# Attention and a routed MoE in one kernel: another cut of the queries, and the second pair's rows made by VectorE instead of TensorE

## The chip, the cores and the metric

The kernel runs on one core of one Trainium2 chip. The time is device time in microseconds, from runs of the whole kernel. Before the change three runs gave 729.36, 731.09 and 735.09 us; the median, 731.09 us, is the time the prediction starts from. One further execution was profiled. It took 731.5 us, of which the trace covers a span of 729.8 us from the first to the last instruction.

The core has five engines that run their own instruction streams in order and wait for one another through semaphores: TensorE (PE in the profile; its weight loads are PEld), VectorE (DVE), ScalarE (ACT), GpSimd (POOL) and SyncE (SP), which issues most DMA transfers.

## The reference

Two blocks follow each other. First attention with a sliding window of 128 keys and a linear distance bias, for 8 batches, 8 heads, 576 positions and head size 64:

```python
scores = scale * np.matmul(q, k.transpose(0, 1, 3, 2))
mask = (rel >= 0) & (rel < window)
scores = np.where(mask, scores + bias[None], -1000000000.0)
attn = np.exp(scores - np.max(scores, axis=-1, keepdims=True))
attn = attn / (np.sum(attn, axis=-1, keepdims=True) + 1e-09)
return np.matmul(attn, v)
```

The result, as 4608 token rows of 512 values, goes through a mixture of experts: a gate picks one of 8 experts for each token, `relu(x @ w1[e]) @ w2[e]` is computed with the picked expert's weights (512 to 1024 to 512), and the row is scaled by the softmax weight of the pick. All of it is in 32-bit floats.

## The kernel before

**Stages.** In the trace, attention takes about the first 178 us; the rest is the experts, one after another. The change lies wholly in attention. The experts need a token's row from main memory (`x_rows`), from which GpSimd gathers the rows of each expert.

**Units and steps.** Attention is cut into 16 units. A unit is a pair of batches and a pair of heads; four units with the same two batches follow each other, and these four are called a pair here (pair 1 is units 0 to 3, pair 2 is units 4 to 7, and so on; in the code `bp` counts them from 0). A unit has 576 queries and keys, that is nine blocks of 64. It is worked off in four steps `g` = 0 to 3, so the main loop (L1389) has 64 steps `i`.

**Scores.** `scores(i)` (L777) handles two key blocks (three in the last step of a unit). TensorE multiplies keys with the up to three query blocks that can see them (L785) into one of two PSUM buffers `sp`; four 64x64 quarters of the array work side by side. ScalarE takes the exponential (L794 for the outer query blocks, L804 for the inner one), and VectorE multiplies the outer part by a precomputed factor of the distance (L798). The product `pe` has six buffers. `scores_to(n)` runs scores up to index n - 1; the main loop keeps it four steps ahead (three in the first two units).

**Values and sums.** `values(u, half, kbs)` (L815) multiplies `pe` by the values (L828) into the accumulator `at`. A unit's queries are taken in two halves, which `QH` (L578) defines: the first five blocks, then the other four. There is a single `at` buffer, so the second half can start only when ScalarE has copied the first away (L845, in `finish`, L836). `finish` also has TensorE form the rows' sums by multiplying `pe` with an indicator (L859) into a buffer `m`, which ScalarE copies or VectorE adds (L870) to `sumT`. `m` has two buffers, which the gates, the transposes and the routing use too.

**The order of a step.** The program order is written out by hand in the main loop (`tc.manual_schedule`); the planner does not move work between steps. Before the change:

- step 0: scores, values of key blocks 0 and 1, a task;
- step 1: values 2 and 3, a task, scores;
- step 2: values 4, finish of the first half, a task, scores, values 3 to 5 of the second half;
- step 3: values 6 to 8, finish of the second half, a task, scores.

**Tasks.** When a pair has been through attention, its gate, routing and rows are made behind the next pair's attention. `behind(bp)` (L1340) returns a list of tasks, and `some()` (L1370) runs one item of it a step. An item can have several parts. Among these parts: `gate` (TensorE and VectorE), `turn` (TensorE transposes, ScalarE copies), `scale_a` to `scale_c` and `count` (VectorE), `place`, `place2`, `ones_at`, `ones_at2`, `enlist` (mostly VectorE), and the rows. In units 10 and 11 every step also runs one of eight VectorE sums of the first expert's weights (`ws_tasks`, L1422, the sums themselves at L530 to L533).

**Rows, two ways.** A pair has 9 row tiles of 128 tokens. Attention's result `xT` lies by column, the row in memory has four pieces of 132 values (128 and 4 scale factors).

1. `row_turned` and `row_out` (L1064, L1073): TensorE transposes four 128x128 blocks (L1067) into `m`, ScalarE copies them to `xs` (L1069), GpSimd adds the scale factors (L1076) and stores the tile with one DMA (L1081; two for the ninth tile).
2. `squares_turned`, `squares_scaled`, `squares_out` (L1116, L1123, L1128): VectorE turns the tile in squares of 32x32 (L1118), GpSimd copies the scale factors (L1126) and stores the tile with four DMAs, one for each 32 partitions (L1137; eight for the ninth tile). The scale factors have first to be brought into the order of the squares, once a pair, by `scales_squared` (L1096 on TensorE, copies on ScalarE).

`xs` has four buffers for both ways (`rows`, L520). Before the change pair 1 uses the second way, pairs 2 and 3 the first, and pair 4, behind the first expert, the second with most stores on SyncE. The ninth tile of pair 1 is made in the third item of pair 2's list.

```python
            ahead = i + (3 if u < 2 else 4)
            if g == 0:
                scores_to(ahead)
```

Of the kernel before, what the change touches and what calls it, by code (L numbers as in the profile page):

```python
# [458 lines left out]
def kernel(  # L459
# [12 lines left out]
    nc = tc.nc  # L472
# [9 lines left out]
    KB = P // 2  # L482
    NK = S // KB
    BP = N // S // 2
    TPB = 2 * S // P
# [21 lines left out]
    with ExitStack() as fast:  # L507
# [70 lines left out]
        QH = [(0, 5 * KB), (5 * KB, 4 * KB)]  # L578
# [761 lines left out]
        def behind(bp):  # L1340
# [10 lines left out]
            if bp == 0:  # L1351
                rt = [lambda t=t: squares_turned(bp, t) for t in range(TPB)]
                ro = [
                    lambda t=t: (squares_scaled(bp, t), squares_out(bp, t, nc.gpsimd)) for t in range(TPB)
                ]
                return [g3[0:1], g3[1:2], g3[2:] + t3[0:1], t3[1:], a, a2, b, b2, c + n, rt[0:1], q + p + rt[1:2],
                        p2 + rt[2:4] + ro[0:2], o + ro[2:4], o2, rt[4:6] + ro[4:5], e + rt[6:8] + ro[5:8]]
            rt, ro = ([lambda t=t, f=f: f(bp, t) for t in range(TPB)] for f in (row_turned, row_out))
            if bp == 1:
                last = [lambda: squares_turned(0, TPB - 1), lambda: squares_scaled(0, TPB - 1),  # L1360
                        lambda: squares_out(0, TPB - 1, nc.gpsimd)]
                return [g3[0:1], g3[1:2], g3[2:] + t3[0:1] + last, t3[1:], a + rt[0:1], a2 + rt[1:2], b + rt[2:3],
                        b2 + rt[3:4], c + n, [], p + ro[0:2], p2 + ro[2:4] + rs[4:5], o + rs[5:6], o2 + rs[6:7], rs[7:8],
                        e + rs[8:9]]
            return [g3, t3, a + a2, b + b2 + rt[0:1], c + n + rt[1:2], rt[2:4], p + p2 + ro[0:4], o + o2 + rs[4:6],
# [23 lines left out]
        for i in range(NG):  # L1389
            u, g = divmod(i, 4)  # L1390
            bp, hp = units[u]
# [13 lines left out]
            if g == 0:  # L1405
                scores_to(ahead)
            if g == 0:
                values(u, 0, (0, 1))
                if u < HP - 1:
                    factors(u + 1)  # L1410
            elif g == 1:
                values(u, 0, (2, 3))
            elif g == 2:
                values(u, 0, (4,))
                finish(u, 0)
                some()
                scores_to(ahead)
                values(u, 1, (3, 4, 5))
            else:
                values(u, 1, (6, 7, 8))  # L1420
                finish(u, 1)
# [5 lines left out]
            if g != 2:  # L1427
                some()
            if g in (1, 3):
                scores_to(ahead)  # L1430
# [322 lines left out]
```

## Time and profile before

| what | value |
|---|---|
| median of three runs | 731.09 us |
| profiled execution | 731.5 us, span 729.8 us |
| TensorE busy | 672.8 us, 92% of the span |
| VectorE busy | 360.8 us, 49% |
| ScalarE busy | 214.0 us, 29% |
| GpSimd busy | 237.2 us, 32% |
| mean granted TensorE clock | 0.966 of full speed |
| data moved | 122.01 MB, 167 GB/s on average |

The busy time of an engine is the time in which one of its instructions runs. The table shows averages over stages that have different limits, so a stage has to be looked at by itself. In the listings by time, a line has the start in us, the duration in us, the engine, the line of the kernel, the operation, what it writes and reads, the shape, how many neighbouring instructions are merged (x40), and in square brackets the idle time of the engine ahead of it and what ended that. A 32-bit matmul shows up as two records, so x16 are eight matmuls. An instruction's end on TensorE is modelled, and neighbours overlap a little; what a stretch of work costs there is best read from its start to the start of the next stretch.

### The profile page before, as it was taken

How to read it: one execution, taken by the hardware profiler on the slowest of the kernel's cores; microseconds unless marked ns; L12 is line 12 of the kernel's file. 1: busy time of each engine (PE TensorE's matmuls, PEld its weight loads, DVE VectorE, ACT ScalarE, POOL GpSimd, SP SyncE). 2: the span in 40 equal slices, each digit the busy share in tenths (PEclk: the TensorE clock that was granted, in tenths of full speed). 3: DMA queues.
4: the chain of work that ended last, by engine and by line, in shares of the span. 5: the costliest groups of instructions: out<-in, count | busy, mean ns of one | idle time of the engine just before them, and what ended most of it. 6: DMA issues, size and time to landing. Idle time of an engine off the chain costs nothing.

```text
span 729.8 us, 14663 instructions
## 1 busy us (share of the span) xinstructions
PE 672.8 (92%) x6004; PEld 551.9 (76%) x6004; DVE 360.8 (49%) x727; ACT 214.0 (29%) x493; POOL 237.2 (32%) x372
## 2 busy tenths in 40 slices
PE   6899899998999849998999799989997998999996
PEld 5678678686888738876878587868786977788893
DVE  3447758673895537422833372347236531842500
ACT  5767467673321211022103111211121021102310
POOL 8000753042025720255027312722271247022020
PEclk9999999999999969998999899989999999999998
DMA  9878988665089603662285318442833472366010
GB/s 267 207 198 250 283 214 264 196 216 165 13 208 335 211 22 116 208 239 53 108 287 169 123 44 285 158 141 72 306 98 130 159 270 55 116 212 222 1 58 8
DMA packets 63167, 122.01 MB, mean 167 GB/s; under 512 B 5905, under 2 KB 29489, under 8 KB 63090
## 3 DMA queue, kind: packets, MB, share of 16 engines
q1 hardware_dynamic: 51138, 92.51, 40.0%
q0 software_dynamic: 10800, 27.58, 12.2%
q8 instruction: 49, 0.80, 0.5%
q10 hardware_dynamic: 1152, 0.88, 0.4%
q14 instruction: 28, 0.23, 0.1%
HBM read 101.79 MB, written 19.96 MB: 167 GB/s over the span
## 4 chain that ended last, share of the span: by engine, by line
PE 61%; issue 19%; another core or an unknown queue 5%; POOL 5%; DVE 3%; ACT 2%; DMA 1%; SPq 0%; POOLq 0%; ACTq 0%; DVEq 0%
PE sp L785 5%; PE at L828 4%; PE pair0b L1558 4%; PE pair0a L1558 4%; PE pair1a L1558 4%; PE pair1b L1558 3%; PE pair0a L1501 3%; POOL xg L1271 3%; PE pair2b L1501 3%; PE pair2a L1501 3%; PE pair0b L1501 3%; PE pair2a L1558 3%; PE pair1a L1501 2%; PE pair2b L1558 2%
## 5 line engine op out<-in xcount | busy, mean ns | idle before, releaser
L1581 POOL DMA_INDIRECT out_dram<-zo,s_idx x39 | 44.4, 1139 | 294.7 <-DVE zo L1572 193.1
L1271 POOL DMA_INDIRECT xg<-x_rows,p_idx x124 | 123.8, 999 | 37.8 <-issue 36.9
L798 DVE TENSOR_TENSOR pe<-pe,fac 128x512 f32<-128x512 f32 x64 | 43.7, 687 | 52.5 <-ACT pe L794 52.5
L785 PE MATMUL sp<-q_sb,k_sb 64*64 64x192 f32 (+2 forms) x1152 | 56.4, 323 | 10.7 <-DMA q_sb<-in_qT_dram 5.3
L828 PE MATMUL at<-pe,v_sb 64*64 64x192 f32 (+2 forms) x1408 | 58.6, 289 | 3.9 <-issue 3.6
L828 PEld LDWEIGHTS at<-pe,v_sb 64*64 64x64 f32 x1408 | 48.3, 137 | 13.9 <-issue 7.9
L785 PEld LDWEIGHTS sp<-q_sb,k_sb 64*64 64x64 f32 x1152 | 40.6, 137 | 19.8 <-issue 8.6
L794 ACT ACTIVATE pe<-sp 128x512 f32<-128x512 f32 x64 | 38.5, 602 | 38.3 <-issue 18.1
L1512 ACT ACTIVATE h<-h 128x512 f32<-128x512 f32 x32 | 20.2, 630 | 89.7 <-DVE h L1511 81.2
L804 ACT ACTIVATE pe<-sp,mid 128x128 f32<-128x128 f32 x128 | 40.2, 374 | 0.0
L859 PE MATMUL m<-pe,ind 128*32 128x192 f32 (+2 forms) x704 | 29.6, 287 | 1.6 <-issue 0.9
L1137 POOL DMA_DIRECT2D x_rows<-xs x48 | 25.9, 549 | 10.3 <-DVE at_col L1023 2.4
L859 PEld LDWEIGHTS m<-pe,ind 128*32 128x32 f32 x704 | 23.2, 110 | 4.0 <-issue 1.1
L1283 DVE TENSOR_TENSOR xn<-xg 128x512 f32<-128x512 f32 x39 | 26.0, 668 | 0.0
L1558 PE MATMUL pair1b<-w,h 128*128 128x256 f32 x72 | 20.2, 405 | 6.1 <-issue 5.9
L1299 DVE STREAM_TRANSPOSE xgT<-xn 128x512 f32<-128x512 f32 x31 | 22.1, 711 | 1.1
L1558 PEld LDWEIGHTS pair1b<-w,h 128*128 128x128 f32 x72 | 14.1, 198 | 10.2 <-issue 8.5
L538 DVE TENSOR_TENSOR w2s<-w 128x512 f32<-128x512 f32 x16 | 10.9, 684 | 21.2 <-DMA w<-in_moe_w_dram 21.2
L845 ACT COPY xT<-at 128x640 f32<-128x640 f32 (+1 forms) x32 | 18.9, 592 | 8.3 <-PE at L828 7.2
L1613 PE MATMUL pair2a<-w,h 128*128 128x512 f32 x48 | 21.1, 592 | 0.0
L1558 PE MATMUL pair2b<-w,h 128*128 128x256 f32 x56 | 16.4, 420 | 4.4 <-issue 4.3
L1558 PE MATMUL pair0b<-w,h 128*128 128x256 f32 x64 | 17.9, 419 | 2.1 <-issue 1.9
(378 smaller groups left out, 1393.4 us busy)
## 6 DMA issues: line engine op xcount, KB each, us to landing
w<-in_moe_w_dram SPq DMA_DIRECT2D x29, 2048.0 KB, 8.0
k_sb<-in_kT_dram SPq DMA_DIRECT2D x15, 576.0 KB, 6.0
q_sb<-in_qT_dram SPq DMA_DIRECT2D x15, 576.0 KB, 6.8
v_sb<-in_v_dram SPq DMA_DIRECT2D x30, 288.0 KB, 4.5
x_rows<-xs POOLq DMA_DIRECT2D x16, 264.0 KB
x_rows<-xs POOLq DMA_DIRECT2D x32, 66.0 KB
x_rows<-xT SPq DMA_DIRECT2D x8, 264.0 KB, 5.8
w<-in_moe_w_dram SPq DMA_DIRECT2D x4, 512.0 KB, 9.4
```

The source lines that it names most:

```text
L785: nc.tensor.matmul(by_distance(sp[c * KB : (c + 1) * KB, r, :GC], kb, 0, n), lhsT=k_sb[u][hs, c, kb * KB : (kb + 1) * KB], rhs=q_sb[u][hs, ...
L794: nc.scalar.activation(outer, sp[:, :, :GC].rearrange("p r (j x) -> p r j x", j=3)[:, :, 0:3:2, :], AF.Exp, scale=SCALE,)
L798: nc.vector.tensor_tensor(outer, outer, fac[:, h0 : h0 + 2, : 2 * w].rearrange("p r (j x) -> p r j x", j=2)[:, :, :, : 2 * KB], op=ALU.mult,)
L804: nc.scalar.activation(pe[:, r, inner], sp[:, r, inner], AF.Exp, bias=mid[:, h0 + r : h0 + r + 1], scale=SCALE,)
L828: nc.tensor.matmul(acc[r * D : (r + 1) * D, c, lo - q0 : hi - q0].rearrange("p (j x) -> p j x", x=KB), lhsT=v_sb[u][c * KB : (c + 1) * KB, ...
L859: nc.tensor.matmul(sm[32 * j : 32 * j + 32, lo - q0 : hi - q0].rearrange("p (j x) -> p j x", x=KB), lhsT=none[:] if pe is None else ind[:, ...
L1137: eng.dma_start(x_d[r0 : r0 + n * m, a * PW : (a + 1) * PW].rearrange("(k i) w -> i k w", i=TQ), xs[a * TQ : (a + 1) * TQ, p0 // TQ : p0 / ...
L1271: nc.gpsimd.indirect_dma_start(out=to, out_offset=None, in_=where, in_offset=bass.IndirectOffsetOnAxis(ap=idx, axis=0),)
L1283: nc.vector.tensor_tensor(xn[:], x, s.unsqueeze(3).to_broadcast([P, NA, HP, TQ]), op=ALU.mult)
L1501: nc.tensor.matmul(ps[:, f * 256 : (f + 1) * 256], lhsT=left[m][:, d, fb * P : (fb + 1) * P], rhs=right[m][:, d, :], start=(m in (1, 2, 5) ...
L1558: nc.tensor.matmul(ps[:, :256], lhsT=left[m][:, f, c * P : (c + 1) * P], rhs=right[m][:, f, :], start=(m in (1, 2, 5) and f == 0), stop=Tr ...
L1581: ins = nc.gpsimd.indirect_dma_start(out=out[:, :], out_offset=bass.IndirectOffsetOnAxis(ap=s_idx[:, g["c0"] + j : g["c0"] + j + 1], axis= ...
```

## The change

Three things change together.

1. The halves are cut elsewhere: the first half has four query blocks, the second five. The first half needs key blocks 0 to 3 and is finished in step 1; the second needs 2 to 8. The number of matmuls and their shapes stay the same in sum.
2. The scores of two steps stand directly behind one another: at the end of step 1 and the start of step 2, and at the end of step 3 and the start of the next step 0. Before, only the latter two were neighbours. A task now runs after all other work of its step, ahead of the scores at the step's end.
3. Pair 2's rows are made the second way, with the same list as pair 1's: no TensorE transposes and ScalarE copies for them, in their place `scales_squared`, VectorE's turns and four GpSimd stores a tile. The eight turns of tiles 1 to 8 fall in units 10 and 11. The ninth tile of pairs 1 and 2 is made in the first item of the next pair's list.

```diff
-        QH = [(0, 5 * KB), (5 * KB, 4 * KB)]
+        QH = [(0, 4 * KB), (4 * KB, 5 * KB)]
...
-            if bp == 0:
+            last = [lambda: squares_turned(bp - 1, TPB - 1), lambda: squares_scaled(bp - 1, TPB - 1),
+                    lambda: squares_out(bp - 1, TPB - 1, nc.gpsimd)] if bp else []
+            if bp < 2:
                 rt = [lambda t=t: squares_turned(bp, t) for t in range(TPB)]
                 ro = [
                     lambda t=t: (squares_scaled(bp, t), squares_out(bp, t, nc.gpsimd)) for t in range(TPB)
                 ]
-                return [g3[0:1], g3[1:2], g3[2:] + t3[0:1], t3[1:], a, a2, b, b2, c + n, rt[0:1], q + p + rt[1:2],
+                return [g3[0:1] + last, g3[1:2], g3[2:] + t3[0:1], t3[1:], a, a2, b, b2, c + n, rt[0:1], q + p + rt[1:2],
                         p2 + rt[2:4] + ro[0:2], o + ro[2:4], o2, rt[4:6] + ro[4:5], e + rt[6:8] + ro[5:8]]
             rt, ro = ([lambda t=t, f=f: f(bp, t) for t in range(TPB)] for f in (row_turned, row_out))
-            if bp == 1:
-                last = [lambda: squares_turned(0, TPB - 1), lambda: squares_scaled(0, TPB - 1),
-                        lambda: squares_out(0, TPB - 1, nc.gpsimd)]
-                return [g3[0:1], g3[1:2], g3[2:] + t3[0:1] + last, t3[1:], a + rt[0:1], a2 + rt[1:2], b + rt[2:3],
-                        b2 + rt[3:4], c + n, [], p + ro[0:2], p2 + ro[2:4] + rs[4:5], o + rs[5:6], o2 + rs[6:7], rs[7:8],
-                        e + rs[8:9]]
-            return [g3, t3, a + a2, b + b2 + rt[0:1], c + n + rt[1:2], rt[2:4], p + p2 + ro[0:4], o + o2 + rs[4:6],
+            return [g3 + last, t3, a + a2, b + b2 + rt[0:1], c + n + rt[1:2], rt[2:4], p + p2 + ro[0:4], o + o2 + rs[4:6],
                     rs[6:9] + [early_holes], e + [early_table, lambda: gather(fixed[0], x_d[: 3 * 2 * S, :])]]
...
-            if g == 0:
+            if g % 2 == 0:
                 scores_to(ahead)
             if g == 0:
                 values(u, 0, (0, 1))
...
             elif g == 1:
                 values(u, 0, (2, 3))
+                finish(u, 0)
             elif g == 2:
-                values(u, 0, (4,))
-                finish(u, 0)
-                some()
-                scores_to(ahead)
-                values(u, 1, (3, 4, 5))
+                values(u, 1, (2, 3, 4, 5))
             else:
                 values(u, 1, (6, 7, 8))
                 finish(u, 1)
...
-            if g != 2:
-                some()
-            if g in (1, 3):
+            some()
+            if g % 2 == 1:
                 scores_to(ahead)
```

## The prediction

> **What bounds the kernel now.** I read the page's busy times and chain, then a table of the attention stage by pair, then TensorE, VectorE, ScalarE and GpSimd in order of time, and last the row tile `xs`. The change lies in attention alone (0 to about 178 us of the span).
>
> ```profile
> PE 672.8 (92%) x6004; PEld 551.9 (76%) x6004; DVE 360.8 (49%) x727; ACT 214.0 (29%) x493; POOL 237.2 (32%) x372
> ...
> PE 61%; issue 19%; another core or an unknown queue 5%; POOL 5%; DVE 3%; ACT 2%; DMA 1%; SPq 0%; POOLq 0%; ACTq 0%; DVEq 0%
> ```
> TensorE is busy 92% of the span and carries 61% of the chain that ended last; VectorE has 3% of it. Over the whole span TensorE looks like the only bound. By stage it is different. Units 4 to 7, 8 to 11 and 12 to 15 carry the routing and row work of the first, second and third pair; in the table by stretch (busy us of PE, PEld, DVE, ACT, POOL, then clock and DMA) they are:
>
> ```profile
> 45.60:88.30 42.70, 38.12 (x891) 30.86 (x886) 28.10 (x69) 25.05 (x68) 11.29 (x24) 0.96 0.87 252
> 88.30:130.70 42.40, 40.32 (x918) 32.27 (x916) 31.30 (x76) 28.40 (x74) 19.72 (x43) 1.00 0.86 246
> 130.70:172.50 41.80, 38.85 (x813) 29.71 (x813) 24.96 (x72) 27.04 (x68) 13.29 (x25) 1.00 0.63 184
> ```
>
> The middle row is where the second pair's rows are made. TensorE is busy 40.3 of 42.4 us, but VectorE already 31.3, most of it in units 9 to 11: units 10 and 11 also carry the eight sums of the first expert's weights (L530 to L533). VectorE's lateness shows there:
>
> ```profile
> 128.04 0.48 DVE L870 TENSOR_TENSOR sumT<-m,sumT 128x320 f32<-128x320 f32 x1
> ...
> 128.57 0.86 PE L859 MATMUL m<-pe,ind 128*32 128x64 f32 x24 [0.77 <-DVE sumT L870]
> ```
>
> VectorE adds a half's sums at 128.04 that TensorE had finished near 125.0, three microseconds earlier. TensorE, wanting that `m` buffer for its next sums, waits 0.77. So before the change VectorE is one step from being the bound.
>
> **Off TensorE.** A row tile's transposes cost TensorE 0.59 us, start to start:
>
> ```profile
> 102.29 0.66 PE L1067 MATMUL m<-ident,xT 128*128 128x128 f32 x4
> 102.88 0.77 PE L828 MATMUL at<-pe,v_sb 64*64 64x192 f32 x16
> ```
>
> Nine of them are 5.3 us: four in unit 9, one in unit 10, four in unit 11. Back comes one turn of the scales into squares, 1.19 us (first pair: 70.19 to 71.38), in unit 10. Net -4.1 us of TensorE. ScalarE loses nine copies of 0.59 and gains two small ones; at 28.4 of 42.4 us busy it was no bound, so nothing is booked.
>
> **On VectorE and GpSimd.** The rows of the tile `xs`:
>
> ```profile
> L1137 POOL DMA_DIRECT2D x_rows<-xs x40: 533/548/598, 72.5 to 102.8; - x40
> L1069 ACT COPY xs<-m x18: 586/586/657, 103.1 to 158.3; 128x512 f32<-128x512 f32 x18
> L1118 DVE STREAM_TRANSPOSE xs<-xT x9: 670/701/712, 69.7 to 95.5; 128x512 f32<-128x512 f32 x9
> ```
>
> VectorE gains nine turns; back to back they start about 0.62 us apart (84.06: two in 1.29). Eight fall in units 10 and 11: 5.0 us. The ninth goes to unit 12. GpSimd issues 40 stores instead of 10: 40 x 0.548 + 9 x 0.5 for the scale copies = 26.4 us, nearer 31.4 with the waits the first pair's had (71.96 to 103.4). From unit 10's third step they end in unit 13. The next pair's rows need GpSimd only in its third step and reuse the four row buffers; by these times both just fit, so I book nothing (if not, up to 2 us through ScalarE's row copy).
>
> A rule speaks against this. The Trainium skill's "SBUF — State Buffer", section "A bandwidth-pool intuition that's wrong", says a DMA issued from GpSimd takes about 3100 ns in place of 620 when it meets a VectorE `tensor_copy` in two-port mode, since GpSimd is locked out of the port. By the rule at its worst, 40 issues are 124 us and the third pair's rows come far too late. But VectorE was busy 60 to 95% of the time from 72 to 103 us and the slowest of 40 issues took 598 ns. I take the row: 22 us for the issues.
>
> **VectorE's sum, the step that decides.** From its first multiply of unit 9 (101.80) to its last addition of unit 11 (end 130.81) VectorE has 29.0 us, of which it waits 0.31 + 0.72 + 0.51 + 0.31 + 1.25 + 0.31 = 3.4. Work: 25.6; with the eight turns 30.6. TensorE needs for the same units after the change 7.2 + 9.1 + 7.8 = 24.1 us (9.9 + 9.1 + 11.5 before, less nine transposes, the 1.6 us of waits and some 0.1 us at each break that a transpose made, plus the squares). So TensorE will outrun VectorE and be held by it: first at values that lack their factors, then at unit 12's gates, whose `m` buffers wait for additions queued behind turns. VectorE starts 1.6 us into unit 9 as before (ScalarE's exp releases it), keeps 0.31 of waiting, and ends at 100.17 + 1.6 + 0.3 + 30.6 = 132.7. Two multiplies (1.2) and the first gate's addition (0.6) follow, then the third gate's matmuls (0.5): gates done at 135.0. Before: 135.05. The 6.4 us that units 8 to 11 would save on TensorE alone (42.4 to about 36.0) thus vanish; what remains is 0.4 us in the rest of unit 12.
>
> **The new order of a unit.** The same matmuls run, in six stretches instead of eight. What it removes is a short wait, seen by comparing a unit without a task in its third step with one that has:
>
> ```profile
> 61.63 0.88 PE L785 MATMUL sp<-q_sb,k_sb 64*64 64x192 f32 x16
> 62.56 1.55 PE L828 MATMUL at<-pe,v_sb 64*64 64x64 f32 x48
> ...
> 106.58 0.88 PE L785 MATMUL sp<-q_sb,k_sb 64*64 64x192 f32 x16
> 107.28 1.50 PE L828 MATMUL at<-pe,v_sb 64*64 64x64 f32 x48
> ```
>
> 0.93 us against 0.70 from scores to values: the one `at` accumulator (L845) has not been copied away yet. After the change two score blocks (1.36 us) lie in between, so the 0.2 goes. Price both ways: 0 where a task lay between or inputs were awaited (units 0 to 2, 4, 8 to 12), 0.2 to 0.3 in units 3, 5, 6, 7 and 13 to 15; a score block that now stands directly ahead of values could also wait for ScalarE, but two `sp` buffers and a half unit (3.6 us) for 2 us of exps cover it. I take 1.3 us. In units 0 and 1, where scores run one block less ahead, the last values follow their own scores by some 1.7 us, about what exp and multiply take (0.6 + 0.7): nothing to -0.5 us, taken as nothing. Moving the last tile's turn two steps earlier puts it ahead of the copy that needs its `xT`: nothing.
>
> **Sum.** Profiled execution 731.5 (span 729.8 and 1.7 around it): -0.4 - 1.3 = -1.7, so 729.8. The median of the runs is 731.09, 0.4 below that execution, so 729.4; I say 729.5.
>
> **Rivals.** *VectorE does not hold TensorE* (it catches up in unit 12, or its turns overlap better than 0.62): the whole 6.4 + 1.3 = 7.7, so 723.4. For it: VectorE is only 49% busy in all. Against: the 0.77 wait above. Chance 0.15.
>
> *The row buffers become VectorE's wait* (slower). Place: the seventh and eighth turn, which need the third and fourth tile's stores landed. The first pair's stores wait for one another too: the third tile's first store came 7.4 us after the first tile's, 3.7 us a tile in place of 2.7. At that pace the fourth tile is issued 14.8 us after the first and lands 3 to 7 us later, up to 5 us after its buffer is wanted, and everything behind that turn on VectorE, the next multiplies and the gates, waits. It decides from 1.7 us of lateness; at 3.5 us the sum is +1.8. TensorE then stands still long enough for the clock to count:
>
> ```profile
> 78.08 0.49 PE L785 MATMUL sp<-q_sb,k_sb 64*64 64x192 f32 x5
> 81.46 0.70 PE L785 MATMUL sp<-q_sb,k_sb 64*64 64x192 f32 x10 [2.89 <-issue]
> ```
>
> After this 2.89 us the granted clock was 0.83 between 80 and 90 us, 3.4 us at half, 1.7 us lost. "TensorE: Matmul & The Clock Gate", Part 1, has the clock halve after an idle window of about 3.4 us; by that the waits here would cost no clock, by the trace 1.7 more. With it and a late third pair (2 us): 731.1 + 1.8 + 1.7 + 2 = 736.6; without the last, 734.6. Chance 0.25.
>
> *The parts miss their aim*: the accumulator was not what was waited for, and VectorE gives all back: 731.1. Chance 0.1.
>
> **How the numbers follow.** The likeliest, 729.5 (its own range 727 to 732), has 0.5. The six waits for "issue" in attention (0.88, 1.29, 0.80, 0.51, 0.60, 2.89) depend on how transfers fall; the largest with its clock is 4.6 us and can go or be doubled, so each case blurs by 2 to 4 us. 80% range: 723.5 to 738. One per cent (7.3 us) is about what a measurement of this kernel can tell from no change: faster 0.12, within 0.70, slower 0.18.
>
> **What would show it.** Right: transposes L1067 gone between 100 and 131 us, unit 9 near 7.2 us; VectorE without idle time from unit 9 to unit 12, TensorE waiting for its multiplies and additions near 120 to 135; forty stores of 0.55 us on GpSimd in place of ten; no 0.2 us ahead of values. Wrong: units 9 to 11 in 24 to 26 us together (VectorE not the bound), VectorE turns that wait for stores, or ScalarE's row copies of the third pair waiting for them; and any change after attention beyond its shift.

## The result: 1.1% slower, and the profile after

The changed kernel took 739.4 us (median of 16 runs), the kernel before 730.4 us beside it. Without the few runs in a slower state of the chip the ratio is 1.0108, with a 95% interval from 1.0082 to 1.0135: about 7.9 us slower. The forecast was 729.5 us with a range up to 738; the result lies just outside it, on the side of the slower rival. The profiled execution took 740.9 us, its span was 739.1 us.

The page after, its busy times and its chain:

```profile
PE 668.9 (90%) x5976; PEld 550.2 (74%) x5976; DVE 366.2 (50%) x736; ACT 210.2 (28%) x486; POOL 254.4 (34%) x402
...
PE 52%; issue 16%; POOL 5%; another core or an unknown queue 4%; DVE 2%; ACT 2%; DMA 1%; POOLq 0%; ACTq 0%; DVEq 0%
```

TensorE has 3.9 us less work, as the sum had it (4.1), and the span is 9.3 us longer. So TensorE stands still or runs slowly somewhere, and the page does not say where. A table by stretches does. Each stretch starts with the first value multiplication of a unit, so that it means the same work in both kernels; the rows are units 4 to 8, 9 to 12, and 13 to 14 (columns as in the prediction's table). Before:

```profile
46.95:101.53 54.58, 49.54 (x1138) 38.70 (x1134) 34.15 (x79) 32.47 (x89) 22.15 (x47) 0.97 0.87 246
101.53:144.31 42.78, 40.88 (x931) 32.86 (x926) 32.93 (x87) 29.59 (x77) 9.98 (x22) 1.00 0.78 229
144.31:165.91 21.60, 21.22 (x475) 17.67 (x468) 14.75 (x46) 15.24 (x39) 9.30 (x20) 1.00 0.64 198
```

After:

```profile
46.18:103.45 57.27, 49.62 (x1138) 38.46 (x1133) 33.80 (x79) 32.55 (x89) 24.07 (x49) 0.94 0.82 240
103.45:147.12 43.67, 37.42 (x903) 31.22 (x899) 36.62 (x91) 25.21 (x70) 22.98 (x47) 0.96 0.74 204
147.12:172.07 24.95, 22.57 (x476) 18.62 (x471) 16.40 (x50) 15.67 (x40) 10.76 (x23) 0.93 0.56 179
```

All three stretches lose: 2.7, 0.9 and 3.4 us. The middle one, which the prediction spent most of its working on, loses least. In all three the granted clock is lower. These are the waits that stand behind the rows, TensorE in order of time:

```profile
92.17 1.93 PE L879 MATMUL m<-xT,wgd 128*32 128x512 f32 x8 [5.32 <-DVE gs L884]
118.59 1.90 PE L859 MATMUL m<-pe,ind 128*32 128x64 f32 x28 [1.22 <-DVE cn L994]
...
132.64 1.92 PE L879 MATMUL m<-xT,wgd 128*32 128x512 f32 x16 [0.72 <-DVE sumT L870]
136.41 0.42 PE L879 MATMUL m<-xT,wgd 128*32 128x128 f32 x8 [1.84 <-DVE gs L884]
...
140.32 0.82 PE L903 MATMUL m<-ident,gs 128*128 128x128 f32 x5 [1.73 <-ACT sumT L868]
```

The three in the middle, 118 to 137 us, are the ones that the forecast had named: VectorE holds TensorE. The last comes from ScalarE and is taken up further down. The first, 5.32 us in unit 8, was not expected. It ends when VectorE has added a gate's product, and VectorE itself had stood still until then, at the first pair's turns (VectorE in order of time):

```profile
80.01 0.70 DVE L1118 STREAM_TRANSPOSE xs<-xT 128x512 f32<-128x512 f32 x1
82.44 0.71 DVE L1118 STREAM_TRANSPOSE xs<-xT 128x512 f32<-128x512 f32 x1 [1.73 <-DMA x_rows<-xs]
85.87 0.71 DVE L1118 STREAM_TRANSPOSE xs<-xT 128x512 f32<-128x512 f32 x1 [2.18 <-DMA x_rows<-xs]
89.63 0.71 DVE L1118 STREAM_TRANSPOSE xs<-xT 128x512 f32<-128x512 f32 x1 [3.05 <-DMA x_rows<-xs]
```

The sixth, seventh and eighth tile need a row buffer whose four stores have not landed: 7.0 us of waiting. Before, the fifth to eighth turn had none:

```profile
84.06 1.29 DVE L1118 STREAM_TRANSPOSE xs<-xT 128x512 f32<-128x512 f32 x2
...
88.60 1.41 DVE L1118 STREAM_TRANSPOSE xs<-xT 128x512 f32<-128x512 f32 x2
```

GpSimd's own rows after show why the stores are late; each bracket is a wait for an earlier store to land before the next can be issued:

```profile
78.16 2.28 POOL L1137 DMA_DIRECT2D x_rows<-xs  x4 [1.86 <-DMA x_rows<-xs]
...
81.81 1.63 POOL L1137 DMA_DIRECT2D x_rows<-xs  x3 [0.33 <-DMA x_rows<-xs]
...
84.73 0.55 POOL L1137 DMA_DIRECT2D x_rows<-xs  x1 [1.08 <-DMA x_rows<-xs]
```

The first pair's stores, from the first copy of scale factors to the last issue, take 30.8 us (70.6 to 101.4); before they took 31.4. They did not get slower; the turns come sooner. The fifth stands 9.4 us after the first copy of scale factors (80.01), before it stood 12.1 us after it (84.06). Part of this is TensorE's stall for "issue" in units 6 and 7, 2.3 us here and 4.0 before.

In unit 13 a third kind of wait appears (all engines in order of time):

```profile
149.10 0.62 PE L859 MATMUL m<-pe,ind 128*32 128x192 f32 x14
...
149.55 1.29 DVE L798 TENSOR_TENSOR pe<-pe,fac 128x512 f32<-128x512 f32 x2
149.64 0.66 PE L1067 MATMUL m<-ident,xT 128*128 128x128 f32 x4
...
151.83 0.40 DVE L870 TENSOR_TENSOR sumT<-m,sumT 128x256 f32<-128x256 f32 x1
152.29 0.69 PE L1067 MATMUL m<-ident,xT 128*128 128x128 f32 x4 [1.99 <-DVE sumT L870]
```

The order of a step now puts `finish` (L859) directly ahead of the task, and this task is two transposes of the third pair. That makes three users of `m` in a row with two buffers. The second transpose needs the sums' buffer, and VectorE's addition that frees it (L870) stands behind two multiplies and five small routing operations: 1.99 us of waiting, and from 152.78 us on the granted clock is at half for 3.4 us. In the kernel before the same two transposes came in a step without a `finish`:

```profile
146.36 1.09 PE L1067 MATMUL m<-ident,xT 128*128 128x128 f32 x8
...
147.38 0.88 PE L785 MATMUL sp<-q_sb,k_sb 64*64 64x192 f32 x16
```

Last, the end of the program. After its last scatter GpSimd drains its queue; the instruction by its line, before:

```profile
L1749 POOLq DRAIN  x3: 46/103/1867, 727.0 to 729.5; - x3
```

and after (minimum, median, maximum in ns):

```profile
L1741 POOLq DRAIN  x3: 46/103/4072, 734.2 to 738.8; - x3
```

The longest of the three went from 1.87 to 4.07 us, and the instruction ahead of it (INC_SWDGE_SEM) from 0.64 to 1.18: 2.7 us more at the very end.

A second trace of both kernels gives units 4 to 8 as 55.80 and 56.26, 9 to 12 as 42.87 and 43.35, 13 to 14 as 21.57 and 24.87. With the means of both pairs of traces the loss is 1.6 + 0.7 + 3.3 + 2.7 = 8.3 us, against 7.9 by the runs. Units 0 to 3, unit 15 and the experts' matmuls differ from execution to execution without a sign that follows the change.

### The profile page after: what moved, and what is told of

It is laid out like the page before. It is cut to its first block, busy times and chain, and to the rows that moved or that the text cites. A ratio compares the mean times of both kernels' runs of the same rounds, so it can differ in the third digit from the quotient of the medians.

```text
span 739.1 us, 14659 instructions
## 1 busy us (share of the span) xinstructions
PE 668.9 (90%) x5976; PEld 550.2 (74%) x5976; DVE 366.2 (50%) x736; ACT 210.2 (28%) x486; POOL 254.4 (34%) x402
## 4 chain that ended last, share of the span: by engine, by line
PE 52%; issue 16%; POOL 5%; another core or an unknown queue 4%; DVE 2%; ACT 2%; DMA 1%; POOLq 0%; ACTq 0%; DVEq 0%
PE pair0b L1550 4%; PE pair0a L1550 4%; PE pair0a L1493 4%; PE pair0b L1493 3%; PE pair1a L1550 3%; PE pair1b L1550 3%; PE pair2a L1550 3%; POOL xg L1271 3%; PE pair2b L1493 3%; PE pair2a L1493 3%; PE pair2b L1550 3%; PE pair1a L1493 3%; PE pair1b L1493 2%; PE pair0a L1605 2%
## 5 line engine op out<-in xcount | busy, mean ns | idle before, releaser
L1573 POOL DMA_INDIRECT out_dram<-zo,s_idx x39 | 44.5, 1141 | 295.1 <-DVE zo L1564 193.4
L1271 POOL DMA_INDIRECT xg<-x_rows,p_idx x124 | 123.9, 999 | 37.8 <-issue 36.6
L798 DVE TENSOR_TENSOR pe<-pe,fac 128x512 f32<-128x512 f32 x64 | 42.8, 686 | 43.2 <-ACT pe L794 43.2
L785 PEld LDWEIGHTS sp<-q_sb,k_sb 64*64 64x64 f32 x1152 | 42.6, 143 | 18.1 <-DMA q_sb<-in_qT_dram 4.2
L828 PE MATMUL at<-pe,v_sb 64*64 64x192 f32 (+2 forms) x1408 | 54.1, 287 | 1.7 <-issue 1.1
L1137 POOL DMA_DIRECT2D x_rows<-xs x88 | 47.7, 550 | 16.3 <-DMA x_rows<-xs 5.6
L828 PEld LDWEIGHTS at<-pe,v_sb 64*64 64x64 f32 x1408 | 46.8, 137 | 7.7 <-issue 3.6
L794 ACT ACTIVATE pe<-sp 128x512 f32<-128x512 f32 x64 | 38.5, 601 | 38.6 <-issue 23.1
L859 PE MATMUL m<-pe,ind 128*32 128x192 f32 (+2 forms) x704 | 31.1, 292 | 5.5 <-issue 4.3
L859 PEld LDWEIGHTS m<-pe,ind 128*32 128x32 f32 x704 | 22.8, 111 | 9.8 <-issue 6.3
L1126 POOL COPY xs<-sq 128x16 f32<-128x16 f32 x19 | 5.4, 282 | 68.5 <-DVE pe L798 53.0
L845 ACT COPY xT<-at 128x512 f32<-128x512 f32 x32 | 19.1, 596 | 21.7 <-DVE xs L1118 13.8
L1299 DVE STREAM_TRANSPOSE xgT<-xn 128x512 f32<-128x512 f32 x31 | 22.1, 712 | 1.1
L1550 PE MATMUL pair2a<-w,h 128*128 128x256 f32 x56 | 18.6, 465 | 4.4 <-issue 3.7
```

What stands on the lines that cost most here:

```text
L785: nc.tensor.matmul(by_distance(sp[c * KB : (c + 1) * KB, r, :GC], kb, 0, n), lhsT=k_sb[u][hs, c, kb * KB : (kb + 1) * KB], rhs=q_sb[u][hs, ...
L794: nc.scalar.activation(outer, sp[:, :, :GC].rearrange("p r (j x) -> p r j x", j=3)[:, :, 0:3:2, :], AF.Exp, scale=SCALE,)
L798: nc.vector.tensor_tensor(outer, outer, fac[:, h0 : h0 + 2, : 2 * w].rearrange("p r (j x) -> p r j x", j=2)[:, :, :, : 2 * KB], op=ALU.mult,)
L828: nc.tensor.matmul(acc[r * D : (r + 1) * D, c, lo - q0 : hi - q0].rearrange("p (j x) -> p j x", x=KB), lhsT=v_sb[u][c * KB : (c + 1) * KB, ...
L859: nc.tensor.matmul(sm[32 * j : 32 * j + 32, lo - q0 : hi - q0].rearrange("p (j x) -> p j x", x=KB), lhsT=none[:] if pe is None else ind[:, ...
L1137: eng.dma_start(x_d[r0 : r0 + n * m, a * PW : (a + 1) * PW].rearrange("(k i) w -> i k w", i=TQ), xs[a * TQ : (a + 1) * TQ, p0 // TQ : p0 / ...
```

## The experiments

The runs fell on several chips. On some the kernel before takes 679 us, on others 729; the experts take 503 us on the one and 549 on the other, attention about the same. So only ratios to the kernel before on the same chip are compared, and lengths of units within attention. The table has one trace for each kernel, in us. "Issue" is TensorE's waiting for nothing that the profile shows, in units 6 and 7; "drain" is GpSimd's longest at the end.

| kernel | ratio (95%) | units 4-8 | issue | 9-12 | 13-14 | drain |
|---|---|---|---|---|---|---|
| before, two traces | 1 | 54.6, 55.8 | 4.0, 5.5 | 42.8, 42.9 | 21.6, 21.6 | 1.87 |
| after, two traces | 1.0108 (1.0082-1.0135); 1.0117 (1.0058-1.0176) | 57.3, 56.3 | 2.3, 3.2 | 43.7, 43.4 | 25.0, 24.9 | 4.07 |
| order alone | 1.0068 (1.0039-1.0098) | 56.1 | 6.6 | 42.7 | 25.0 | 1.87 |
| rows alone | 1.0095 (1.0072-1.0119) | 54.8 | 1.8 | 45.7 | 22.1 | 4.07 |
| after, eight buffers | 1.0035 (1.0013-1.0057) | 51.5 | 4.1 | 42.8 | 23.3 | 4.07 |
| after, weight sums later | 1.0152 (1.0107-1.0197) | 56.1 | 2.9 | 44.5 | 24.5 | 4.07 |
| after, task before finish | 1.0092 (1.0066-1.0117) | 56.3 | 3.3 | 42.9 | 23.0 | 4.07 |
| the same, eight buffers | 1.0042 (1.0016-1.0067) | 56.9 | 7.7 | 42.8 | 22.6 | 4.07 |
| order, buffers, parted | 1.0029 (1.0002-1.0056) | 51.8 | 2.9 | 45.0 | 24.6 | 1.87 |
| after, parted | 1.0151 (1.0112-1.0191) | 56.4 | 5.9 | 43.4 | 24.8 | 4.07 |
| after, buffers, sums later, parted | 0.9991 (0.9971-1.0010) | 51.0 | 3.1 | 40.1 | 23.1 | 4.07 |

**The two halves of the change.** First the new order without the new rows; the main loop is that of the change (the first pair's ninth tile has to move along, since its `xT` is wanted two steps sooner):

```diff
-        QH = [(0, 5 * KB), (5 * KB, 4 * KB)]
+        QH = [(0, 4 * KB), (4 * KB, 5 * KB)]
...
-                return [g3[0:1], g3[1:2], g3[2:] + t3[0:1] + last, t3[1:], a + rt[0:1], a2 + rt[1:2], b + rt[2:3],
+                return [g3[0:1] + last, g3[1:2], g3[2:] + t3[0:1], t3[1:], a + rt[0:1], a2 + rt[1:2], b + rt[2:3],
...
-            if g == 0:
+            if g % 2 == 0:
                 scores_to(ahead)
...
                 values(u, 0, (2, 3))
+                finish(u, 0)
...
```

> The kernel before with the new order of a unit alone (cut of the queries, scores in twos, finish of the first half in step 1); the second pair's rows stay on TensorE, the first pair's ninth tile is made in the first item of the second pair's list. If the order alone, by bringing the first pair's turns up to its stores sooner (row buffers), makes the new stall: VectorE's turns at 82 to 90 us wait 1.7 to 3 us each for stores, TensorE stands about 5 us and some 7 us are run at half clock, and units 8 to 11 lose what units 4 to 7 gained: about 731 to 735 us. If the loss is VectorE's overfull time with the second pair's turns: no stall worth speaking of, and the order's gain stays, 725 to 729 us.

It measured 1.0068, about 4.6 us slower: neither of the two. The first pair's turns waited little (0.59 and 1.66 us); in this execution TensorE stood 6.6 us for "issue" in units 6 and 7, which gave the stores time. But unit 13 has the new wait, within a hundredth of the changed kernel's 1.99 us (TensorE in order of time):

```profile
147.76 0.66 PE L1067 MATMUL m<-ident,xT 128*128 128x128 f32 x4
150.40 0.66 PE L1067 MATMUL m<-ident,xT 128*128 128x128 f32 x4 [1.98 <-DVE sumT L870]
```

So the loss in units 13 and 14 (25.0 for 21.6 us) comes from the order and has nothing to do with the second pair's rows. The new order, priced at a gain of 1.3 us, is a loss by itself.

Then the rows without the order:

```diff
-            if bp == 0:
+            if bp < 2:
...
-                return [g3[0:1], g3[1:2], g3[2:] + t3[0:1], t3[1:], a, a2, b, b2, c + n, rt[0:1], q + p + rt[1:2],
+                return [g3[0:1], g3[1:2], g3[2:] + t3[0:1] + last, t3[1:], a, a2, b, b2, c + n, rt[0:1], q + p + rt[1:2],
...
-            return [g3, t3, a + a2, b + b2 + rt[0:1], c + n + rt[1:2], rt[2:4], p + p2 + ro[0:4], o + o2 + rs[4:6],
+            return [g3 + last, t3, a + a2, b + b2 + rt[0:1], c + n + rt[1:2], rt[2:4], p + p2 + ro[0:4], o + o2 + rs[4:6],
```

> The kernel before with the second pair's rows made in squares alone; the order of a unit is the old one. If VectorE, full with turns and the weight sums in units 9 to 12, is the loss: TensorE waits for VectorE at 118 to 141 us as in the changed kernel, 735 to 738 us. If the loss is the first pair's turns that wait for stores, which the new order brings about: no such waits here at 82 to 90 us, 729 to 732 us.

1.0095, about 6.5 us, at the upper end of what a full VectorE would give; but only 2.9 of it lie in units 9 to 12. The rest was in neither theory: the drain is 4.07 us here too (with INC_SWDGE_SEM 2.7 us more), while the order alone has 1.87. And the first pair's turns waited even with the old order:

```profile
86.10 0.71 DVE L1118 STREAM_TRANSPOSE xs<-xT 128x512 f32<-128x512 f32 x1 [1.22 <-DMA x_rows<-xs]
89.61 0.71 DVE L1118 STREAM_TRANSPOSE xs<-xT 128x512 f32<-128x512 f32 x1 [2.80 <-DMA x_rows<-xs]
```

That refutes the expectation that only the new order brings these waits about. TensorE's stalls in units 6 and 7 were short here (1.8 us). Both count, as the traces with four buffers and GpSimd's stores show together. In the old order stalls of 1.8 us went with 5.3 us of waiting turns, and 3.2 to 5.5 us with 0 to 0.4. In the new order 2.3 to 3.3 us of stalls went with 3.8 to 7.2 us of waiting, and 5.9 and 6.6 us with 2.3. What brings the turns up to the stores sooner, the order or a shorter stall, makes them wait.

**Row buffers.** Tiles 4 to 7 of the first two pairs go to a scratch tile that attention does not use:

```diff
...
+                elif bp < 2 and 4 <= t < 8:
+                    if bp not in more:
+                        more[bp] = mx_pool.tile([P, NJ, NA, PW], F32, name="xg")
+                    xs_of[bp, t] = more[bp][:, t - 4]
```

> The changed kernel with eight row buffers in place of four for the first and second pair, so that no turn of these pairs' tiles 1 to 8 waits for a store. Row buffers as the cause: the three waits of 1.7 to 3.1 us on VectorE go, and with them TensorE's 5.3 us and most of the 6.8 us at half clock; stage of units 8 to 11 from 47.2 to about 40, whole kernel 731 to 734 us. VectorE's work as the cause: the stall goes but units 9 to 12 take the time back, 737 to 740 us.

1.0035 in place of 1.011: some 5 us come back. No turn waits any more, units 4 to 8 fall to 51.5 us, which is 3 us below the kernel before. The row of these units, to be read beside those above:

```profile
46.34:97.79 51.45, 47.28 (x1137) 37.44 (x1133) 34.13 (x79) 32.43 (x89) 18.85 (x39) 1.00 0.87 250
```

The clock is 1.00 where it was 0.94. Of the 3 us, 1.7 are the half-clock stretch that the trace of before has in these units (0.97) and this one has not. So the row buffers cost the changed kernel not only a small loss against before, but the order's gain in these units. What is left above the kernel before is units 13 and 14 (1.7 us) and the drain.

**Weight sums later.** The eight sums leave units 10 and 11:

```diff
-            if u in (10, 11):
+            if u in (13, 14):
```

> The changed kernel with the eight weight sums of the first expert (2 x 4 on VectorE, in units 10 and 11) moved to units 13 and 14. VectorE's work as the cause: units 10 to 12 lose the waits of TensorE for VectorE (1.2, 0.7, 0.7, 1.8, 1.7 us) and a half clock of 3.4 us, 733 to 735 us. Row buffers of the first pair as the cause: the stall of 5.3 us in units 7 and 8 stays, and the time with it, 738 to 740 us.

1.0152: not the 733 to 735 us of a VectorE that is short of time. The first pair's turns still waited (0.98, 2.44 and 2.45 us), as the other expectation has it. Units 9 to 12 did not gain (44.5 us), because VectorE, freed of the sums, ran into the stores of the second pair:

```profile
130.81 0.71 DVE L1118 STREAM_TRANSPOSE xs<-xT 128x512 f32<-128x512 f32 x1 [3.08 <-DMA x_rows<-xs]
132.61 0.71 DVE L1118 STREAM_TRANSPOSE xs<-xT 128x512 f32<-128x512 f32 x1 [1.08 <-DMA x_rows<-xs]
```

So the second pair meets both limits that the prediction had weighed against one another: first VectorE's work, and once that is less, the row buffers.

**Both kernels again on one chip, and the neighbours in unit 13.** The kernel before once more, for its trace:

> The kernel before again, for its trace beside the other runs of this chip. If what the experiments so far show lies in attention and in the end of the program, and not in the chip: experts about 503 us from the first expert matmul to the end, as with the order alone (502.9), attention 175 us; the last wait of GpSimd 1.87 us.

The experts took 548.8 us, not the expected 503: the chip is one of those on which they take longer. Attention (its first 9.2 us included) took 179.5. The drain was 1.87 us as expected. The changed kernel:

> The changed kernel again, for its trace and time beside the other runs of this chip. All theories: 1.008 to 1.014 times the kernel before, as on the first chip. Row buffers: three turns of the first pair wait for stores near 82 to 90 us. The new order: the transposes of the third pair in unit 13 wait about 2 us for VectorE's addition of sums. The end: GpSimd's last wait 4.07 us in place of 1.87, as in all kernels with 40 more stores by GpSimd and unlike the order alone.

1.0117; the turns wait 1.81, 2.57 and 2.79 us, the transposes in unit 13 1.92, the drain is 4.07: all as in the first trace. In the next kernel the two transposes are made before `finish`:

```diff
             elif g == 1:
                 values(u, 0, (2, 3))
+                if u in (13, 14):
+                    some()
                 finish(u, 0)
...
-            some()
+            if g != 1 or u not in (13, 14):
+                some()
```

> The changed kernel with the task of step 1 ahead of the finish of the first half in units 13 and 14 alone, so that the third pair's two transposes in that step find both buffers m free of a sum that VectorE has yet to add. If the new neighbours finish and transposes are a cause: the wait of 2 us in unit 13 and the half clock behind it go, -2 to -3.7 us against the changed kernel on this chip. If the wait only shows that VectorE is late there anyway: the next user of m waits as long, 0 to -1 us.

1.0092 against 1.0117 of the changed kernel, on the same chip; the intervals overlap, so the time alone settles nothing. The trace, a single one, shows it: units 13 and 14 take 23.0 us for 24.9, the wait on the addition is gone, no clock is lost. Not all is gained, since ScalarE now makes the row copies before it copies `at`:

```profile
152.04 1.22 PE L828 MATMUL at<-pe,v_sb 64*64 64x64 f32 x32 [1.15 <-ACT xT L845]
```

> The changed kernel with the task ahead of the finish in units 13 and 14 and with eight row buffers for the first two pairs. If both are causes and add up: 2 to 3.7 us below the changed kernel with eight buffers alone (1.0035 times before), so 0.998 to 1.001 times before, with the longer end of the program still in it. If they share one cause (VectorE's lateness), no more than the buffers alone: 1.003.

1.0042, 3.6 us below the same kernel with four buffers: the row buffers a second time, on one chip. But it is not below 1.0035, the eight buffers alone on another chip: the expectation that the two edits add up is not met. The traces leave little to add. With eight buffers alone unit 13 had its wait but no half clock (why, the last section shows), so units 13 and 14 took 23.3 us, and the swap brings them to 22.6.

**The end of the program.** Two kernels keep the rows of before and only split stores, so that GpSimd issues 24 and 6 DMAs more. The edit of the first; the second cuts six tiles in halves:

```diff
-                nc.gpsimd.dma_start(x_d[r0 : r0 + n, :], xs[p0 : p0 + n].rearrange("p a w -> p (a w)"))
+                w = n // 4 if bp == 1 and t < TPB - 1 else n
+                for b in range(0, n, w):
+                    nc.gpsimd.dma_start(x_d[r0 + b : r0 + b + w, :], xs[p0 + b : p0 + b + w].rearrange("p a w -> p (a w)"))
```

> The kernel before; the second pair's tiles 1 to 8 are still made by TensorE, but each is stored by four DMAs of 32 rows in place of one of 128, 24 more by GpSimd; the bytes are the same. If GpSimd's last wait grows with the number of DMAs it has issued: about 3.6 us (1.87 + 24/30 of 2.2). If it hangs on which of the eight semaphores the last DMA has, which 24 more leave as it was: 1.87 us. If it hangs on the layout in squares: 1.87 us.

> The kernel before; six of the second pair's tiles are stored in two halves, 6 more DMAs by GpSimd, so that the last DMA falls on the same one of the eight semaphores as in the changed kernel. If the number counts: about 2.3 us for GpSimd's last wait. If the semaphore counts: 4.07 us. If the layout counts: 1.87 us.

The drain of the first:

```profile
L1751 POOLq DRAIN  x3: 46/103/3173, 681.6 to 685.4; - x3
```

and of the second:

```profile
L1751 POOLq DRAIN  x3: 46/103/1867, 675.1 to 677.5; - x3
```

So it is neither the layout in squares alone (24 more stores of whole rows lengthen it) nor the semaphore of the last DMA, of which GpSimd's DMAs use eight in turn (6 more leave the drain as it was). The whole kernels took 687.4 and 679.5 us, one run each, beside 679.2 before; the first also loses 6 us in unit 11, where ScalarE's row copies now wait for stores, the longest time 3.59 us.

Nothing hides the drain. On the chips where the experts take some 503 us, their length follows it: 502.8 and 502.9 us with a drain of 1.87, 504.5 with 3.17, 505.5 to 505.7 with 4.07.

**Transposes parted.** The third pair's two transposes go into two steps:

```diff
-            return [g3 + last, t3, a + a2, b + b2 + rt[0:1], c + n + rt[1:2], rt[2:4], p + p2 + ro[0:4], o + o2 + rs[4:6],
+            return [g3 + last, t3, a + a2, b + b2 + rt[0:1], c + n + rt[1:2], rt[2:3], rt[3:4] + p + p2 + ro[0:4], o + o2 + rs[4:6],
```

With the order alone and eight buffers for the first pair:

> The kernel before with the new order alone, eight row buffers for the first pair, and the third pair's two transposes of unit 13's step 1 parted into steps 1 and 2; the second pair's rows by TensorE. If the row buffers and the new neighbours in unit 13 make the loss of the order alone (1.0068): no wait of transposes for VectorE's addition in unit 13, no wait of the first pair's turns, 0.997 to 1.001 times before. If the order costs elsewhere (its stalls for instructions): 1.003 to 1.007.

1.0029. Unit 13 falls to 10.9 us, as before the change, and unit 14 takes it back, 13.7 for 10.7: there the transposes wait for ScalarE's row copies, which wait for stores. Units 9 to 12 lose 2.2 us as well (45.0): TensorE waits 0.71 and 1.74 us for the second pair's row copies, and the clock is at 0.96.

```profile
159.09 0.66 PE L1067 MATMUL m<-ident,xT 128*128 128x128 f32 x4 [2.24 <-ACT xs L1069]
```

In the changed kernel alone the split does the same and gains nothing:

> The changed kernel; the only edit parts the third pair's two transposes of unit 13's step 1 into steps 1 and 2. If three users of m in a row (sums, transpose, transpose) make the loss in unit 13: that unit falls from 14.7 us to about 11, and the kernel is 2 to 3.7 us below the changed one (1.0114 times before on average so far): 1.006 to 1.009. If ScalarE's row copies wait for row buffers then, the time is lost again in unit 14 as with the order alone and the split: 1.010 to 1.012.

1.0151, with 24.8 us for units 13 and 14; the theory that the loss can be taken out by moving one transpose is refuted, the one that it moves on to unit 14 holds. All three remedies together:

> The changed kernel with eight row buffers, the weight sums in units 13 and 14, and the two transposes of unit 13 parted. If VectorE's work in units 9 to 12 holds TensorE: those units, 42.8 us with eight buffers alone, take 38 to 40; then 0.995 to 1.000 times before, the longer end of the program included. If the sums only move the wait (units 13 and 14 take back what 9 to 12 gain): 1.002 to 1.005.

0.9991 (0.9971 to 1.0010). With the stores no longer in the way, later sums do what they were meant to: units 9 to 12 take 40.1 us, of which 2.3 are a stall for "issue".

```profile
98.76:138.81 40.05, 36.61 (x902) 30.53 (x898) 32.14 (x83) 25.28 (x70) 26.86 (x55) 1.00 0.87 246
```

VectorE is busy 32.1 of 40.1 us there, in the changed kernel 36.6 of 43.7. So its work was a bound in these units, as forecast, but taking it away pays only once the row buffers are out of the way. The kernel is as fast as the one before, not faster; the drain eats 2.7 us of what attention gains.

**Stores by SyncE.** To tell GpSimd's pace from the transfers', the first two pairs' stores were issued by SyncE, those of the ninth tiles likewise:

```diff
-                    lambda t=t: (squares_scaled(bp, t), squares_out(bp, t, nc.gpsimd)) for t in range(TPB)
+                    lambda t=t: (squares_scaled(bp, t), squares_out(bp, t, nc.sync)) for t in range(TPB)
```

> The changed kernel with the stores of the first two pairs' rows issued by SyncE in place of GpSimd; four row buffers as in the changed kernel. If GpSimd's pace with its stores (31 us for a pair) is what the turns wait for: the turns' waits near 82 to 90 us go or shrink to under 1 us each, units 4 to 8 fall from 57 to 52 us; and GpSimd, with some 80 DMAs less, ends with a wait of 1.87 us or less: 1.000 to 1.003 times before. If the transfers themselves are slow, or SyncE's own loads stand in the way: the turns wait as before, 1.008 or more.

1.0418 (1.0382 to 1.0454). The turns wait no less (2.65, 0.34 and 4.58 us), and TensorE waits for queries, whose loads SyncE issues in order behind the stores:

```profile
111.00 2.84 PE L785 MATMUL sp<-q_sb,k_sb 64*64 64x192 f32 x32 [3.48 <-DMA q_sb<-in_qT_dram]
```

It answers the question only by half: SyncE is no place for these stores, but whether the transfers would be faster from another queue stays open. With the three remedies in place the same happens:

> The changed kernel with eight row buffers, the weight sums in units 13 and 14, the two transposes parted, and the stores of the first two pairs by SyncE: all causes found taken away. If they add up: the version without SyncE's stores (0.9991) less the longer end of 2.7 us (0.4%), 0.993 to 0.996 times before. If SyncE's loads come late by it, 0.998 or more.

1.0386. The drain, with 50 DMAs fewer than before, is 6.77 us in both. That refutes the count as such. Two last kernels, both with the three remedies and GpSimd's stores, bring the count near that of before with the stores still in squares, the first by storing tiles 4 to 7 together:

```diff
+        def four_out(bp, eng):
...
+            (p0, m, r0), = placed(bp, 4)
+            for a in range(NA):
+                eng.dma_start(
+                    x_d[r0 : r0 + 4 * m, a * PW : (a + 1) * PW].rearrange("(k i) w -> i k w", i=TQ),
+                    more[bp][a * TQ : (a + 1) * TQ].rearrange("p t k w -> p (t k) w"),
+                )
```

> The version with eight row buffers, later weight sums and the parted transposes (0.9991 times before); tiles 4 to 7 of the first two pairs are now stored together, by four DMAs instead of sixteen, so that GpSimd issues 247 DMAs in all, as many as the kernel with six more than before. If the longer end hangs on the count of GpSimd's DMAs (241 and 247: 1.87 us, 265: 3.17, 271: 4.07, 191: 6.77): 1.87 to 2 us, the end 2.7 us shorter, 0.994 to 0.997 times before. If it hangs on the way of storing (squares): 4.07 us and 0.998 to 1.000.

The second has, besides, the ninth tile stored by four DMAs of 32 whole rows in place of eight of pieces (the source is `xs[:, k, :]` for each 32 rows `k`):

> As the version with tiles 4 to 7 stored together; besides, the ninth tile of the first two pairs is stored by four DMAs of 32 whole rows instead of eight of 32 pieces: 239 DMAs by GpSimd. By the count: 1.87 us or less for GpSimd's last wait, 0.994 to 0.997 times before. By the way of storing: 4.07 us, 0.998 to 1.000.

0.9989 (0.9969 to 1.0009) and 1.0026 (1.0004 to 1.0048). The drain is 3.83 us with 247 DMAs, where 247 gave 1.87 above, and 5.30 us with 239; the experts take 505.3 and 507.1 us with it, and 508.9 in the two kernels with 6.77. So the end hangs on none of the three things tried (count, semaphore, layout in squares) alone. It is fixed for a set of stores: all nine traces of kernels that keep the changed kernel's stores by GpSimd, on several chips, have 4.07 us, and those of the kernel before and the two with its stores untouched 1.87. What law it follows stays open. No version beat the kernel before.

## Why the prediction was wrong

**Right: TensorE's and VectorE's work, and units 9 to 12.** The step "VectorE's sum, the step that decides" had the gates of unit 12 done at 135.0 us, 33.5 after the start of unit 9; they were done at 136.83, 33.4 after it. The sum behind it holds too: VectorE was to be through with eight turns 32.5 us after the scores ahead of unit 9 began (100.17 to 132.7), and was so after 32.5 (102.09 to 134.56), with 0.8 us of waiting. TensorE lost the 5.3 us of transposes, was held by VectorE near 118 to 137 us, and the 6.4 us that it could have saved vanished as worked out. That this was no accident the kernel with eight buffers and later sums shows, where these units fall to 40.1 us. What units 9 to 12 lose beyond the forecast lies behind the gates, at the ninth tile's turn (below).

GpSimd's issues were read rightly against the rule that spoke against them: the 88 stores of the changed kernel took 536 to 601 ns each. The share given for VectorE beside them was too high, though. Before the change it was busy 74% of the time from 72 to 90 us and 44% from 90 to 103, not 60 to 95%.

**Wrong: "The new order of a unit", priced at -1.3 us.** The price came from what the order removes, 0.2 us of waiting for `at`. That wait did go: in unit 5, with no task in its third step, 7.52 us became 7.23. With eight buffers units 4 to 8, less their "issue" stalls and half the time at half clock, take 46.8 to 48.0 us in the traces, in the old order, where no turn waited over 0.5 us, 48.6 to 49.7. By this estimate the order does gain some 1.7 us there, median against median. What failed is that only the removed neighbours were looked at, not the new ones. `finish`, moved to step 1, now stands ahead of the third pair's two transposes, and a task with two `m` tiles behind a sum that VectorE must free first makes a wait. Units 13 and 14: +3.3 us, about half of it the wait, half the clock. The kernel with the order alone shows it apart from the new rows, and with the task ahead of `finish` 1.9 us of it go.

**Wrong: "so I book nothing" for the row buffers, and with it "Moving the last tile's turn two steps earlier puts it ahead of the copy that needs its `xT`: nothing".** The rival had the right mechanism, the seventh and eighth turn waiting for stores, but at the second pair. The forecast said nothing of the first pair's turns, which the change does not touch. Yet it speeds up the TensorE work that leads to them. In the kernel before, the old order and TensorE's stalls in units 6 and 7 gave the stores time. The last tile's turn, now in the first item of the next list, stands behind these waits, and the copy of `xT` behind it waited 7.2 us in unit 8; for the second pair the same turn waited 1.42 us for its store, and TensorE 1.73 us for the copies behind it. The loss against before is small (+1.6 us in units 4 to 8, 0.7 in 9 to 12), because shorter stalls (2.0 us less by the means of both traces) and the order's own gain stand against it. What was really missed is what eight buffers bring back by the runs: 3.6 us on one chip, some 5 across two.

**A term too small: the clock.** The likeliest sum had no loss of clock in it, and the rival counted one stretch of 3.4 us at half clock. The trace after has one of 6.8 us (unit 8) and two of 3.4 (units 10 and 13), that of before one of 3.4. The loss of clock by the table's rows is 0.06 x 57.3 + 0.04 x 43.7 + 0.07 x 24.95 = 6.9 us after and 0.03 x 54.6 = 1.6 before; the second traces have 5.1 and 1.7. Not all of it is lost time: the stretch in unit 10 lies where VectorE held TensorE anyway, and without it the second trace is only 0.3 us shorter in units 9 to 12. By the rule of an idle window of 3.4 us that the prediction set against its trace, the waits of 1.22 and 1.99 us should have cost no clock; the clock was at half behind both, so the trace of before was the better guide (more in the last section).

**Not seen: the end.** "1.7 around" the span and everything behind attention were carried over unchanged. The drain's 2.7 us are a third of the loss, and no reason for them stood in the trace of before. Among the signs of being wrong the prediction had "any change after attention beyond its shift"; this is one.

## What to carry to other kernels

When work is put into another order, write down for each moved step who uses the same few buffers just ahead of it and behind it, and which engine frees them: the price lies in the new neighbours, not in the wait that goes. A stage that speeds up must be followed to the next thing it runs into at its old pace, also in parts that the change leaves alone; here the old order and a stall had covered the first pair's stores. And look at the last microseconds of the trace as a stage of its own whenever the number or shape of GpSimd's DMAs changes.

## What was unexpected of the hardware

The drain of GpSimd at the end took 1.87, 3.17, 3.83, 4.07, 5.30 or 6.77 us, the same in every trace of one set of stores, and neither rising nor falling with the number of DMAs.

A single wait of TensorE of 1.98 to 1.99 us was followed by 3.4 us at half clock in the changed kernel and in the order alone; the same wait in unit 13 of the kernel with eight buffers left the clock at 1.00:

```profile
145.78 0.66 PE L1067 MATMUL m<-ident,xT 128*128 128x128 f32 x4 [1.98 <-DVE sumT L870]
```

So the length of one wait does not decide by itself. How it falls does. In each trace here the changes of the clock lie on a grid of 3.413 us. In the changed kernel the whole wait lies in one cell of this grid (columns as in the first table; the clock is the third figure from the end):

```profile
149.37:152.78 3.41, 1.42 (x22) 1.01 (x13) 2.74 (x9) 1.24 (x3) 0.66 (x2) 1.00 0.41 97
152.78:156.19 3.41, 3.41 (x54) 2.71 (x56) 0.69 (x1) 2.03 (x5) 2.37 (x7) 0.50 0.95 313
```

With eight buffers a border at 144.29 us cuts the wait in two, and no cell stands idle for longer than 1.49 us:

```profile
140.88:144.29 3.41, 2.92 (x60) 2.06 (x52) 3.17 (x12) 3.04 (x9) 0.90 (x2) 1.00 0.61 214
144.29:147.70 3.41, 1.92 (x36) 1.69 (x40) 1.33 (x7) 1.10 (x3) 1.74 (x5) 1.00 0.66 204
147.70:151.11 3.41, 3.41 (x96) 2.91 (x86) 2.63 (x9) 2.54 (x8) 1.59 (x4) 1.00 0.97 296
```

Counted over attention from 20 us on, in all 19 traces and for cells at full clock: where no matmul ran for 1.9 us or more of a cell, 33 of 34 were followed by one at half clock; with 1.72 to 1.9 us, 7 of 12; with less, 4 of 793. The cell with unit 10's wait of 1.22 us is one of these four, for which the record has no reason.

The stalls for "issue" in units 6 and 7 lay between 1.8 and 7.7 us. Between one execution and another they make up to 5.9 us, nearly as much as the whole change does.
